# Which engine copies which accumulator at the end of a chunk, in an FFT and feed-forward kernel

## The chip, the cores and the metric

The kernel runs on one core of a Trainium2 chip. The metric is the device time of one execution in microseconds; a version is represented by the median of several runs. Lower is better. Five engines work side by side, each through its own queue in order: TensorE (PE in the profile; its weight loads are PEld), VectorE (DVE), ScalarE (ACT), GpSimd (POOL) and SyncE (SP), which issues most of the DMA transfers.

## The reference

The input `x` has shape 8 x 3008 x 256. The reference takes a two-dimensional Fourier transform over the last two axes, keeps the real part, and sends each of the 24064 rows through a feed-forward layer:

```python
X = np.fft.fft(np.fft.fft(x, axis=1), axis=2).real
h = X.reshape(-1, 256) @ w_in            # 256 -> 2048
g = where(h >= 1, h, where(h <= -1, 0, (h + 1)**2 / 4))
out = g @ w_out                          # 2048 -> 256
```

## The kernel before

The kernel splits the length 3008 into 64 x 47 and makes the transform of a batch by two stages of matmuls (`stage1`, `stage2`); the second transform is folded into `w_in`. Rows s and -s of the result are the sum and the difference of the same two products, so that only half of the rows is multiplied, and each product serves two signs (`sg` is 0 or 1). A batch has three chunks of columns, 482, 512 and 512 wide (`WIDTH`), and a chunk is worked through in 16 steps over the 2048 hidden features, 128 at a time. One such step is a unit `(b, k, f)`: batch, chunk, block of features. The first chunk of a batch is called narrow below, the other two wide.

For a unit, `gemm1` makes two products in PSUM (`uv`, three banks, six matmuls, L425). VectorE makes from them the two signs of h (`us` L428, `h` L430 and L431), ScalarE the square of the shifted half (`a`, L435 and L436), VectorE the activation (L447), ScalarE its high part (`gh`, L450) and POOL the low part (`gl`, L453). Four units later `gemm2` multiplies both parts with `w_out` (L485) and adds the products up in four PSUM accumulators of a bank each, `acc0` to `acc3`. Accumulator `dh * 2 + sg` holds half `dh` of the 256 output features for sign `sg`, and `gemm2` fills them in this order, three matmuls each. They are summed over the 16 units of a chunk. At the last unit the four sums are copied to SBUF (`o`), by VectorE (L496) or ScalarE (L494), and stored, one store for each `dh` (L503). The next chunk starts by overwriting the same four banks, so its first matmul into a bank waits until that bank's copy is over. Between the two stand the six `uv` matmuls of one unit and, in most batches, one piece of the next batch's FFT (`s`, L315 or L388).

The first batch differs. Its chunks are worked first over four units and later over the other twelve, while the weights are still being prepared. After the four units the sums are stored as parts (L501); after the twelve, VectorE adds the loaded parts to the accumulators (L492), all four of them.

What sets the order: for the first 24 units the order on each engine is pinned as written. After that the framework's scheduler orders each engine's queue when the program is built, by priority and by modelled times at which operands are ready. The copies are traced with a priority 150 steps ahead (`EVICT_AHEAD`), so that they may be queued ahead of work that is written earlier. FFT pieces of the next batch are spread over the units (`fft_pieces`), and the loads of x for it stand in SP's queue between the stores; POOL (and at times VectorE) adds them up (`fold_x`, L136 and L140).

Of the kernel before, what the change touches and what calls it, by code (L numbers as in the profile page):

```python
# [113 lines left out]
def fft_ffn_kernel(ctx: ExitStack, tc: tile.TileContext, x, cst, w_in, w_out, out):  # L114
# [296 lines left out]
    n_units = len(units)  # L411
# [50 lines left out]
    def gemm2(i):  # L462
        b, k, f = units[i]
        n = WIDTH[k]
        act = acts.pop(i)
        half_way = b == 0 and f == FIRST - 1
        begin, last = f == 0 or (b == 0 and f == FIRST), half_way or f == NFT - 1
        if begin:
            for j in range(4):
                accs[j] = ps.tile([P, CH], F32, tag=f"acc{j}", name=f"acc_{i}_{j}", bufs=1)  # L470
        for dh in range(2):
            wc = slice(dh * P, (dh + 1) * P)
            add = (k, dh) in outs if b == 0 else False
            if last:
                o = outs.pop((k, dh)) if add else sb.tile([P, 2, CH], F32, tag="o", name=f"o_{i}_{dh}", bufs=2)
            for sg in range(2):
                acc = accs[dh * 2 + sg]
                if i < NATIVE:
                    wo_at = (f % 2) * D + dh * P
                    terms = [(wo32[f // 2][:, wo_at : wo_at + P], act[0])]  # L480
                else:
                    gh, gl = act
                    terms = [(wo[t][:, f, wc], g) for t, g in (("woh", gh), ("wol", gh), ("woh", gl))]
                for j, (w, g) in enumerate(terms):
                    nc.tensor.matmul(  # L485
                        acc[:, :n], w, g[:, sg], start=(begin and j == 0), stop=(last and j == len(terms) - 1)
                    )
                if last:

                    with tc.high_priority(offset=EVICT_AHEAD):  # L490
                        if add:
                            nc.vector.tensor_tensor(o[:, sg, :n], acc[:, :n], o[:, sg, :n], op=ALU.add)  # L492
                        elif sg:
                            nc.scalar.activation(o[:, sg, :n], acc[:, :n], AF.Copy)  # L494
                        else:
                            nc.vector.tensor_copy(o[:, sg, :n], acc[:, :n])  # L496
                    if i == n_units - 1:
                        nc.sync.dma_start(out[b, k, dh, sg, :, :n], o[:, sg, :n])
            if half_way:
                parts[k, dh] = dr.tile([P, 2, CH], F32, tag="part", name=f"part_{k}_{dh}", bufs=6)  # L500
                nc.sync.dma_start(parts[k, dh][:, :, :n], o[:, :, :n])  # L501
            elif last and i < n_units - 1:
                nc.sync.dma_start(out[b, k, dh].rearrange("s p t -> p s t")[:, :, :n], o[:, :, :n])  # L503
# [75 lines left out]
    for i in range(n_units + LAG):  # L579
# [18 lines left out]
        if 2 <= i < PINNED and i not in SKIP:  # L598
            gemm2(second)
            second += 1  # L600
# [11 lines left out]
        if i >= PINNED:  # L612
            gemm2(second)
            second += 1
# [57 lines left out]
```

## Time and profile before

| | |
|---|---|
| median of 3 runs | 1746.41 us (1745.89 to 1746.51) |
| profiled execution | 1746.05 us |
| its span, first to last instruction | 1744.3 us |
| granted TensorE clock | 1.000 |
| copies on VectorE, L496 | 48, mean 672 ns, 32.0 us in all |
| copies on ScalarE, L494 | 48, mean 580 ns, 26.8 us in all |
| additions of the first batch on VectorE, L492 | 12, mean 676 ns, 7.5 us in all |
| L447 on VectorE | 360, mean 1518 ns |
| L450 on ScalarE | 360, mean 1045 ns |

A row of the waits names the waiting engine and line, what released it, the total in us, the number of times and the longest. A row in order of time gives the start in us, the duration in us, engine, line and operation, output and inputs, shape, and in brackets the idle time ahead of it and what ended that. A matmul is drawn longer than the distance to the next one, because matmuls overlap in the array and their ends are modelled; a merged row ends in the number of instructions that it holds. A wait for several things is put down to the one that came last.

### The profile page before, as it was taken

To read this page: it belongs to the slowest core of one execution; us is meant where nothing else is said; L and a number is where in the kernel's file an instruction comes from. 1 tells how busy PE (TensorE), PEld (TensorE's weight loads), DVE (VectorE), ACT (ScalarE), POOL (GpSimd) and SP (SyncE) were. 2 spreads that over 40 slices of the span, in tenths; PEclk is the share of its full clock that TensorE was granted. 3 is DMA by queue.
4 is the path that set the end of the run, shared out by engine and by line. 5 is a ranking of instruction groups with operands and counts; after the bars stand their busy time and mean duration, and the time that the engine had idled before them with its cause. 6 is when DMAs were issued, how large, how long until landed. Compare 5 with 4: busy or idle time off the path is not lost.

```text
span 1744.3 us, 21532 instructions
## 1 busy us (share of the span) xinstructions
PE 1729.2 (99%) x7818; PEld 1391.7 (80%) x7818; DVE 1419.8 (81%) x1752; ACT 1335.4 (77%) x1560; POOL 1156.8 (66%) x805
## 2 busy tenths in 40 slices
PE   9999999999999999999999999999999999999998
PEld 6556888888888888888888888887888878887876
DVE  7997788888887888777887888877888788788886
ACT  6877777877778777787777777778777787777775
POOL 1125867776678766777667766677666766667666
PEclk9999999999999999999999999999999999999999
DMA  8133112110011000110011100111001010000000
GB/s 316 47 108 130 57 48 73 48 37 31 13 61 59 31 25 23 50 59 31 25 46 39 59 19 25 49 37 59 31 13 37 1 36 31 0 25 24 1 25 25
DMA packets 33738, 80.89 MB, mean 46 GB/s; under 512 B 4704, under 2 KB 9952, under 8 KB 33632
## 3 DMA queue, kind: packets, MB, share of 16 engines
q1 hardware_dynamic: 33596, 79.52, 13.2%
q8 instruction: 61, 1.00, 0.2%
q14 instruction: 45, 0.37, 0.1%
q10 hardware_dynamic: 36, 0.01, 0.0%
HBM read 51.70 MB, written 27.81 MB: 46 GB/s over the span
## 4 chain that ended last, share of the span: by engine, by line
PE 65%; ACT 14%; DVE 8%; POOL 7%; issue 6%; DMA 0%; ACTq 0%; POOLq 0%; SPq 0%
PE acc L485 40%; PE uv L425 20%; POOL gl L453 7%; DVE h L447 6%; ACT a L436 5%; ACT gh L450 5%; ACT a L435 3%; PE s L315 2%; PE s L388 2%; PE wps L278 1%; DVE h L430 1%; ACT z L345 0%; DVE h L431 0%; DMA x<-in_x_dram 0%; POOL y L136 0%
## 5 line engine op out<-in xcount | busy, mean ns | idle before, releaser
L453 POOL TENSOR_TENSOR gl<-h,gh 128x512 fp32r<-128x512 f32 (+1 forms) x720 | 1034.0, 1458 | 441.9 <-ACT gh L450 413.0
L447 DVE SCALAR_TENSOR_TENSOR h<-a,h 128x1024 f32<-128x1024 f32 (+1 forms) x360 | 546.5, 1518 | 226.8 <-ACT a L436 225.5
L450 ACT ACTIVATE gh<-h 128x1024 fp32r<-128x1024 f32 (+1 forms) x360 | 376.1, 1045 | 345.9 <-DVE h L447 316.5
L485 PE MATMUL acc<-gh,woh 128*128 128x512 f32 (+1 forms) x1440 | 570.5, 396 | 4.5 <-DVE o L496 3.1
L485 PE MATMUL acc<-gl,woh 128*128 128x512 f32 (+1 forms) x1440 | 563.9, 392 | 0.9 <-POOL gl L453 0.9
L485 PE MATMUL acc<-gh,wol 128*128 128x512 f32 (+1 forms) x1440 | 560.8, 389 | 0.0
L435 ACT ACTIVATE a<-h,biases 128x1024 f32<-128x1024 f32 (+1 forms) x384 | 431.7, 1124 | 26.2 <-DVE h L431 24.1
L436 ACT ACTIVATE a<-a 128x1024 f32<-128x1024 f32 (+1 forms) x384 | 398.9, 1039 | 7.8
L485 PEld LDWEIGHTS acc<-gh,woh 128*128 128x128 f32 x1440 | 270.7, 188 | 63.9 <-DVE o L496 6.3
L485 PEld LDWEIGHTS acc<-gl,woh 128*128 128x128 f32 x1440 | 271.3, 188 | 58.6 <-POOL gl L453 2.2
L485 PEld LDWEIGHTS acc<-gh,wol 128*128 128x128 f32 x1440 | 270.7, 188 | 54.7
L425 PE MATMUL uv<-pqh,wh 128*128 128x512 f32 (+1 forms) x768 | 310.7, 405 | 1.6 <-DVE h L431 0.9
L430 DVE TENSOR_TENSOR h<-us,uv 128x512 f32<-128x512 f32 (+1 forms) x384 | 259.8, 677 | 62.5 <-POOL gl L453 20.6
L425 PE MATMUL uv<-pql,wh 128*128 128x512 f32 (+1 forms) x768 | 299.0, 389 | 0.0
L425 PE MATMUL uv<-pqh,wl 128*128 128x512 f32 (+1 forms) x768 | 298.9, 389 | 0.0
L428 DVE SCALAR_TENSOR_TENSOR us<-nyb,delta,uv 128x512 f32<-128x512 f32 (+1 forms) x384 | 279.2, 727 | 16.7 <-PE uv L425 16.6
L431 DVE TENSOR_TENSOR h<-us,uv 128x512 f32<-128x512 f32 (+1 forms) x384 | 256.4, 668 | 0.0
L425 PEld LDWEIGHTS uv<-pqh,wh 128*128 128x128 f32 x768 | 144.2, 188 | 45.8 <-DVE h L431 6.7
L425 PEld LDWEIGHTS uv<-pqh,wl 128*128 128x128 f32 x768 | 144.2, 188 | 33.6 <-issue 5.4
L425 PEld LDWEIGHTS uv<-pql,wh 128*128 128x128 f32 x768 | 144.1, 188 | 30.1 <-DVE pql L174 0.2
L136 POOL TENSOR_TENSOR y<-x 96x512 f32<-96x512 f32 x60 | 106.0, 1769 | 27.9 <-DMA x<-in_x_dram 15.9
L345 ACT ACTIVATE z<-s 64x192 f32<-64x192 f32 x242 | 82.2, 340 | 4.8 <-PE s L315 1.0
(65 smaller groups left out, 681.8 us busy)
## 6 DMA issues: line engine op xcount, KB each, us to landing
x<-in_x_dram SPq DMA_DIRECT2D x64, 512.0 KB, 3.5
out_dram<-o SPq DMA_DIRECT2D x26, 512.0 KB, 2.8
out_dram<-o SPq DMA_DIRECT2D x14, 482.0 KB, 2.9
nyb<-nyr SPq DMA_DIRECT2D x24, 256.0 KB, 3.2
raw<-in_moe_w_in_dram SPq DMA_DIRECT2D x4, 512.0 KB, 7.3
raw<-in_moe_w_out_dram SPq DMA_DIRECT2D x4, 512.0 KB
part<-o SPq DMA_DIRECT2D x4, 512.0 KB
os<-part SPq DMA_DIRECT2D x4, 512.0 KB, 5.8
```

Source lines behind the costliest of these rows:

```text
L136: first = engine.tensor_tensor(y, t[:96, 0], t[:96, 1], op=ALU.add)
L345: ins = nc.scalar.activation(dst, src, AF.Copy)
L425: nc.tensor.matmul(t[:, :n], w[m][:, cols], r[:, m, :n], start=(j == 0), stop=(j == 2))
L428: nc.vector.scalar_tensor_tensor(us, nyb[b, k][:, :n], delta[:, f : f + 1], uv[0], op0=ALU.mult, op1=ALU.add)
L430: nc.vector.tensor_tensor(h[:, 0], us, uv[1], op=ALU.subtract)
L431: nc.vector.tensor_tensor(h[:, 1], us, uv[1], op=ALU.add)
L435: nc.scalar.activation(a, h, AF.Relu, bias=half, scale=0.5)
L436: nc.scalar.activation(a, a, AF.Square)
L447: nc.vector.scalar_tensor_tensor(h, a, 1.0, h, op0=ALU.min, op1=ALU.max)
L450: nc.scalar.activation(gh, h, AF.Copy)
L453: nc.gpsimd.tensor_tensor(gl[:, sg], h[:, sg], gh[:, sg].bitcast(F32), op=ALU.subtract)
L485: nc.tensor.matmul(acc[:, :n], w, g[:, sg], start=(begin and j == 0), stop=(last and j == len(terms) - 1))
```

## The change

At the end of a chunk VectorE copied acc0 and acc2 (`sg` 0) and ScalarE acc1 and acc3 (`sg` 1). After the change VectorE copies acc0 and acc3, ScalarE acc1 and acc2. The very last unit of the kernel keeps the old division, and the additions of the first batch are untouched. This concerns 23 chunk ends: the three half-way ones of the first batch and 20 of the 21 chunks of the other seven.

```diff
                     with tc.high_priority(offset=EVICT_AHEAD):
                         if add:
                             nc.vector.tensor_tensor(o[:, sg, :n], acc[:, :n], o[:, sg, :n], op=ALU.add)
-                        elif sg:
+                        elif sg != (0 if i == n_units - 1 else dh):
                             nc.scalar.activation(o[:, sg, :n], acc[:, :n], AF.Copy)
                         else:
                             nc.vector.tensor_copy(o[:, sg, :n], acc[:, :n])
```

## The prediction

> **What bounds the kernel now.** I read the page first, then the list of waits, then the same list for the copies and their neighbours alone, then the instructions in order of time around single chunk changes. The page says that PE (TensorE) is busy all the time:
>
> ```profile
> span 1744.3 us, 21532 instructions
> ...
> PE 1729.2 (99%) x7818; PEld 1391.7 (80%) x7818; DVE 1419.8 (81%) x1752; ACT 1335.4 (77%) x1560; POOL 1156.8 (66%) x805
> ```
>
> A busy PE only shows that it has little room, not that it sets the pace. The list of waits (total us, times, longest) shows who waits for whom:
>
> ```profile
> ACT gh L450 <- DVE h L447: 316.5, 257, 2.7
> DVE h L447 <- ACT a L436: 225.5, 313, 2.7
> ...
> DVE us L428 <- PE uv L425: 16.6, 25, 2.4
> ...
> PE acc L485 <- DVE o L496: 3.1, 9, 0.7
> ```
>
> VectorE (DVE) and ScalarE (ACT) wait for each other hundreds of times; VectorE waits for a finished uv bank of TensorE 25 times in all. Asked of L428, the first VectorE step behind each pair of uv banks, for 500 to 1735 us alone, the view of one line gives:
>
> ```profile
> L428 DVE SCALAR_TENSOR_TENSOR us<-nyb,delta,uv x281: 702/734/745, 499.3 to 1725.3; 128x512 f32<-128x512 f32 x96, 128x482 f32<-128x482 f32 x45
> ...
> its engine sat idle before it (us, times) until:
> who waited for it (us, times):
>   PEld uv L425: 3.6, 11
> ```
>
> Nothing stands under "sat idle before it": in 281 units VectorE never once stood idle for TensorE here, while TensorE's weight loads waited 11 times for VectorE. The last L428 starts at 1725.3, so all 25 of those waits lie before 500 us. From 500 us on the pace is set by the loop L430, L431 (VectorE), L435, L436 (ScalarE), L447 (VectorE), L450 (ScalarE), L453 (POOL), and TensorE runs beside it with little to spare. A wait that TensorE loses is worth its time only where TensorE is about to fall behind that loop; a step that leaves the loop is worth its time wherever the loop has no other wait.
>
> **What is moved.** The copies that lie in 500 to 1735 us, by the view of their two lines:
>
> ```profile
> L496 DVE COPY o<-acc x34: 646/678/686, 552.7 to 1677.5; 128x512 f32<-128x512 f32 x22, 128x482 f32<-128x482 f32 x12
> ```
>
> ```profile
> L494 ACT ACTIVATE o<-acc x34: 557/579/601, 553.5 to 1678.7; 128x512 f32<-128x512 f32 x22, 128x482 f32<-128x482 f32 x12
> ```
>
> Two copies on each engine at each of 17 chunk changes, before and after: nothing is added or removed on either engine. The third accumulator (acc2) goes from VectorE to ScalarE, the fourth (acc3) the other way. Acc2 is complete three matmuls before acc3, and the next chunk wants it three matmuls earlier. What counts is where the second copy stands in each queue, and there are two pictures. The first is the change from the narrow chunk (482 columns) to the next one; ScalarE, VectorE, then TensorE:
>
> ```profile
> 552.42 1.04 ACT L436 ACTIVATE a<-a 128x1024 f32<-128x1024 f32 x1
> 553.49 1.04 ACT L494 ACTIVATE o<-acc 128x482 f32<-128x482 f32 x2
> 555.04 1.06 ACT L450 ACTIVATE gh<-h 128x1024 fp32r<-128x1024 f32 x1 [0.52 <-DVE h L447]
> ```
>
> ```profile
> 552.74 0.65 DVE L496 COPY o<-acc 128x482 f32<-128x482 f32 x1
> 553.50 1.45 DVE L447 SCALAR_TENSOR_TENSOR h<-a,h 128x1024 f32<-128x1024 f32 x1
> 554.88 0.65 DVE L496 COPY o<-acc 128x482 f32<-128x482 f32 x1
> ```
>
> ```profile
> 554.90 0.39 PE L485 MATMUL acc<-gl,woh 128*128 128x512 f32 x1
> 555.58 0.50 PE L485 MATMUL acc<-gh,woh 128*128 128x512 f32 x1 [0.28 <-DVE o L496]
> ```
>
> ScalarE makes its two copies back to back, 553.49 to 554.53. VectorE's second copy stands behind L447 and ends at 555.53; TensorE, which wants acc2, starts at 555.58. The second picture is a change between wide chunks, again ScalarE, VectorE, TensorE:
>
> ```profile
> 624.52 0.58 ACT L494 ACTIVATE o<-acc 128x512 f32<-128x512 f32 x1
> 626.30 1.06 ACT L450 ACTIVATE gh<-h 128x1024 fp32r<-128x1024 f32 x1 [1.20 <-DVE h L447]
> 627.26 0.58 ACT L494 ACTIVATE o<-acc 128x512 f32<-128x512 f32 x1
> 627.74 1.14 ACT L435 ACTIVATE a<-h,biases 128x1024 f32<-128x1024 f32 x1
> ```
>
> ```profile
> 624.65 1.56 DVE L447 SCALAR_TENSOR_TENSOR h<-a,h 128x1024 f32<-128x1024 f32 x1
> 626.13 0.68 DVE L496 COPY o<-acc 128x512 f32<-128x512 f32 x1
> 626.73 0.67 DVE L431 TENSOR_TENSOR h<-us,uv 128x512 f32<-128x512 f32 x1
> ```
>
> ```profile
> 627.19 0.40 PE L485 MATMUL acc<-gl,woh 128*128 128x512 f32 x1
> 627.42 0.40 PE L485 MATMUL acc<-gh,woh 128*128 128x512 f32 x1
> ```
>
> Here ScalarE's second copy stands behind L450 and pushes L435, the next step of the loop, to 627.74, although its input (L431) is there at 627.40. TensorE starts on acc2 at 627.42 without a wait: VectorE's copy is over at 626.81.
>
> **Each part, with its cost.** Narrow changes: TensorE's matmuls follow each other by 0.23 us (627.19 to 627.42), so 554.90 to 555.58 holds a loss of 0.68 - 0.23 = 0.45 us. If ScalarE copies acc2 in the second of its two places, acc2 is free at 554.53, and the loss goes. Next in line is acc3, wanted at 555.13 + 3 x 0.23 = 555.8 and free on VectorE at 555.53: no new wait. The loop gains nothing here, since ScalarE's pair stood ahead of L450 already and VectorE's place is the same.
>
> Wide changes: acc2 is ready three matmuls (0.7 us) before acc3 was. ScalarE stands idle for 1.20 us ahead of L450, so I expect the copy of acc2 in that gap, at about 625.0 to 625.6, with L450 still at 626.30, held by L447. Then L435 starts when L431 is done, at about 627.42 instead of 627.74: 0.32 us off the loop. It would be 0.47 if VectorE also put L431 ahead of its copy of acc3 (L435 then starts right behind L450, at 627.27), and nothing if the copy stayed behind L450. I take 0.32, the case that leaves VectorE's order as it is. It lies on the path because nothing else holds L435.
>
> The two changes of this kind in the last part, where there are no FFT pieces, are alike:
>
> ```profile
> 1544.74 0.58 ACT L494 ACTIVATE o<-acc 128x512 f32<-128x512 f32 x1
> 1545.22 1.09 ACT L435 ACTIVATE a<-h,biases 128x964 f32<-128x964 f32 x1
> ```
>
> ```profile
> 1544.26 0.64 DVE L431 TENSOR_TENSOR h<-us,uv 128x482 f32<-128x482 f32 x1
> ```
>
> L431 ends at 1544.90, so L435 gains 0.30 there. At the four changes that begin batches 3 to 6 (694, 906, 1118 and 1330 us) the gain is lost again: POOL stands for x from memory before it can feed the loop, and that fetch starts when POOL's own earlier step frees the buffer.
>
> ```profile
> 704.77 0.32 POOL L140 TENSOR_TENSOR yd<-x 96x64 f32<-96x64 f32 x1 [3.55 <-DMA x<-in_x_dram]
> ```
>
> The stores: the second one of a chunk waits for acc2 and acc3, and can leave up to 1.0 us earlier (626.81 instead of 627.84). Nobody gains: behind it in SP's queue stand loads that wait for POOL.
>
> ```profile
> SPq L128 <- POOL y L136: 750.0, 51, 56.4
> ```
>
> The changes before 500 us: three half-way ones in the first batch, where each engine makes both copies in a row and the order is fixed by hand, and three at 340, 412 and 482 us, where TensorE does not wait for a copy (the list for 500 to 1735 us alone has all nine waits for L496, 3.1 us). I cost them at nothing; what hides them is the FFT or weight matmuls that stand between two chunks there, and without that cover each would cost the 0.45 us above.
>
> The sum, for the loop: the wide changes inside batches at 624, 836, 1048, 1260 and 1471 us give 5 x 0.32 = 1.6 us, and those at 1541 and 1675 us 0.30 + 0.32 = 0.6; together 2.2 us. TensorE must follow. It loses 0.45 us at each narrow change now, and that goes, so it has 0.45 us more per batch while the loop asks for 0.32. The profiled execution took 1746.05 us, with 1.75 us around its span; 1746.05 - 2.2 = 1743.85. The median of the runs, 1746.41, is 0.36 above it, so the forecast for the median is 1744.2 us. With 0 and 0.47 in place of 0.32 the same sum gives 1746.4 and 1743.1.
>
> **Rival 1, TensorE is the bound after all.** Then every wait for acc2 counts. The nine waits for L496 sum to 3.1 us; each hides another 0.16 us (a matmul is drawn 0.39 long and followed after 0.23), which makes 4.5. One of the nine is for acc0, which stays on VectorE, 0.17 + 0.16 = 0.3:
>
> ```profile
> 1541.82 0.45 PE L485 MATMUL acc<-gh,woh 128*128 128x482 f32 x1 [0.17 <-DVE o L496]
> ```
>
> So 4.2 us go, and the time is 1742.2. For it speaks 99% busy; against it the empty list before L428. The Trainium skill (Trainium Kernel Development and Optimization, Performance Expectations) calls matmul busy time a bad metric for the distance to the limit, since matmuls are pipelined; the drawn 0.39 against a spacing of 0.23 agrees, and by it the 99% is no evidence for this rival.
>
> **Rival 2, nothing moves.** The copy of acc2 stays behind L450 at wide changes, or another wait of the loop takes up the 0.3 us: the loop's own waits above are 225.5 / 313 = 0.7 and 316.5 / 257 = 1.2 us each, and one of them need only grow. TensorE's gain at narrow changes and its loss at wide ones (acc2 free at 627.84, wanted at 627.42) cancel. The time is 1746.4, give or take 1.
>
> **Rival 3, slower.** The copy of acc2 is queued behind L450 at every change, narrow ones too. ScalarE keeps its order: ahead of 626.30 it stood idle for 1.20 us with a copy queued behind L450. Behind L450 a copy starts 0.1 us before L450's end (627.26), so acc2 is free at 556.0 + 0.58 = 556.6 at a narrow change instead of 555.53, 1.06 us more; at a wide change 627.84, 0.5 us late. With TensorE falling behind the loop, five of each make 5 x 1.06 + 5 x 0.5 = 7.8 us: 1754.2. It decides as soon as L450 stands ahead at the narrow changes; at wide ones alone it is rival 2. For it: L450 is ahead of ScalarE's second copy at wide changes now. Against it: acc2 is ready earlier than acc3, and the copies carry a raised priority. The Trainium skill (PSUM — Partial Sum Buffer, Engine vs sequencer instructions) says that the queues of these engines are strict FIFO; the 1.20 us ahead of L450 agrees. By that rule the copy pays for whatever stands ahead of it, and the change would be the 7.8 us slower if the order came out so.
>
> **How the numbers follow.** A measurement of this kernel can tell about 0.2% (3.5 us) from no change. Forecast: 0.48, of which a quarter goes to times under 1742.9, because L431 may also move and TensorE's own gain may add to it. Rival 1: 0.20, faster. Rival 2: 0.14, the same. Rival 3, with any other reordering of the loop that costs it one more wait per change: 0.18, slower. So faster is 0.20 + 0.12 = 0.32, the same 0.36 + 0.14 = 0.50, slower 0.18. The range leaves out rival 3 and reaches from a little below rival 1, 1741.8, to rival 2 with its 1 us and some, 1748.0.
>
> **What would show it.** Right: at 624 us and its four repeats ScalarE has its two copies together ahead of L450, and L435 starts 0.3 us after L450 ends or sooner; TensorE's waits for L496 fall from nine to four or fewer; the list before L428 gets a few waits for TensorE of 0.1 to 0.3 us. Wrong: L450 between ScalarE's two copies; waits of TensorE for L494 of about 1 us; L435 as late as now; or an order of the loop between two chunk changes that isn't the one of now, which no step above prices.

## The result and the profile after

The kernel after takes 1737.59 us (median of 5 runs, 1735.25 to 1739.35), the kernel before, run beside it, 1746.31 us (5 runs, 1744.97 to 1746.51): 8.7 us less, ratio 0.995, 95% interval 0.9939 to 0.996. The profiled execution took 1735.65 us, at a granted clock of 1.000. The forecast had 1744.2 us with a range of 1741.8 to 1748.0: the sign was right, the size was not, and the result lies below the range.

The page of the kernel after, its first lines:

```profile
span 1733.9 us, 21505 instructions
...
PE 1723.4 (99%) x7818; PEld 1394.8 (80%) x7818; DVE 1414.6 (82%) x1752; ACT 1332.6 (77%) x1560; POOL 1174.8 (68%) x805
```

The busy times hardly moved (VectorE 5 us less, ScalarE 3, POOL 18 more): no work left the kernel, so what changed is the waiting. The list of waits of the kernel after:

```profile
ACT gh L450 <- DVE h L447: 311.5, 285, 2.8
DVE h L447 <- ACT a L436: 234.4, 309, 2.2
...
DVE us L428 <- PE uv L425: 11.6, 13, 2.4
...
DVE h L430 <- POOL gl L453: 5.3, 8, 1.1
...
PE acc L485 <- DVE o L496: 1.8, 5, 0.6
```

TensorE's waits for a copy went from nine to five, against four or fewer in the forecast. Of the waits "POOL yd L140 <- DMA x", 15.7 us in five before, the four at the batch starts (14.6 us) are gone; one of 1.2 us before 300 us is left. The view of L428 for 500 to 1735 us in the kernel after has nothing under "sat idle before it" again, so TensorE still doesn't hold up VectorE:

```profile
L428 DVE SCALAR_TENSOR_TENSOR us<-nyb,delta,uv x280: 700/734/740, 502.4 to 1715.3; 128x512 f32<-128x512 f32 x96, 128x482 f32<-128x482 f32 x44
...
its engine sat idle before it (us, times) until:
who waited for it (us, times):
  DVE h L430: 1.0, 2
  PEld uv L425: 0.7, 3
```

The narrow change of the kernel after, TensorE in order of time; the first row overwrites acc1, the third acc2:

```profile
553.91 0.39 PE L485 MATMUL acc<-gh,woh 128*128 128x512 f32 x1
...
554.37 0.40 PE L485 MATMUL acc<-gl,woh 128*128 128x512 f32 x1
554.61 0.39 PE L485 MATMUL acc<-gh,woh 128*128 128x512 f32 x1
```

554.61 - 554.37 = 0.24: the 0.45 us that TensorE lost there before acc2 is gone, as forecast. The wide change of the kernel after, ScalarE and then VectorE:

```profile
623.23 1.07 ACT L494 ACTIVATE o<-acc 128x512 f32<-128x512 f32 x2
625.01 1.06 ACT L450 ACTIVATE gh<-h 128x1024 fp32r<-128x1024 f32 x1 [0.71 <-DVE h L447]
625.97 1.13 ACT L435 ACTIVATE a<-h,biases 128x1024 f32<-128x1024 f32 x1
```

```profile
623.36 1.55 DVE L447 SCALAR_TENSOR_TENSOR h<-a,h 128x1024 f32<-128x1024 f32 x1
624.83 0.67 DVE L431 TENSOR_TENSOR h<-us,uv 128x512 f32<-128x512 f32 x1
625.43 0.68 DVE L496 COPY o<-acc 128x512 f32<-128x512 f32 x1
```

ScalarE makes both copies ahead of L450 (before: one ahead, one behind), VectorE has L431 ahead of its second copy (before: behind), and L435 follows L450 at once, 2.74 us after the first copy's start; before that was 627.74 - 624.52 = 3.22. The last part looks the same (ScalarE in the kernel after):

```profile
1533.50 1.07 ACT L494 ACTIVATE o<-acc 128x512 f32<-128x512 f32 x2
1535.18 1.01 ACT L450 ACTIVATE gh<-h 128x964 fp32r<-128x964 f32 x1 [0.62 <-DVE h L447]
1536.10 1.09 ACT L435 ACTIVATE a<-h,biases 128x964 f32<-128x964 f32 x1
```

And POOL at the start of a batch, where it stood 3.55 us for x before:

```profile
698.92 2.23 POOL L136 TENSOR_TENSOR y<-x 96x512 f32<-96x512 f32 x1
701.40 3.33 POOL L453 TENSOR_TENSOR gl<-h,gh 128x482 fp32r<-128x482 f32 x2 [0.24 <-ACT gh L450]
704.81 0.32 POOL L140 TENSOR_TENSOR yd<-x 96x64 f32<-96x64 f32 x1
```

A pair of L453 now stands between L136, whose end releases the fetch of x, and yd (L140), which needs that x. The wait is covered.

The loads of x wait for POOL as before (SyncE's own queue in the kernel after):

```profile
SPq L128 <- POOL y L136: 745.2, 51, 56.7
```

POOL's move is not in the diff. When the two copies changed engines, the framework's scheduler put the queues of VectorE and ScalarE in another order at about 420 places, 33 of them with a copy in them and the others between the changes, mostly exchanges of neighbours (L431 with L447, L435 with L450), and moved yd on POOL at four batch starts. TensorE's and SyncE's queues stayed the same. Between the first copy (52.2 and 52.1 us) and the end of the span the kernel after is 10.3 us shorter. To see where they lie, take the start of VectorE's first copy at each chunk end, and the difference from one to the next. Stretch a lies between the ends of the narrow and the first wide chunk of a batch, b between those of the two wide chunks, c is the narrow chunk of the next batch, in which yd stands; each is the mean of three batches, 553 to 1189 us before. "Narrow, no yd" is the narrow chunk from 1331 to 1400 us before, which is like c but has no yd in it; "last" is what follows up to the end of the last narrow chunk, 1400 to 1607 us:

| kernel | a | b | c | narrow, no yd | last |
|---|---|---|---|---|---|
| before | 71.18 | 70.33 | 70.55 | 69.25 | 207.16 |
| after | 71.64 | 69.98 | 69.02 | 69.31 | 203.78 |
| copies ahead alone (below) | 71.14 | 70.02 | 71.60 | 68.73 | 206.63 |
| POOL's move alone | 71.17 | 70.34 | 69.55 | 69.24 | 207.12 |
| both | 71.21 | 70.01 | 69.65 | 68.76 | 206.64 |
| both, and L431 ahead | 71.04 | 69.81 | 69.30 | 68.60 | 206.47 |

The kernel after is 1.5 us faster in c, 0.35 in b, 3.4 in the last stretch, and 0.46 slower in a. The forecast had b, and 0.6 us of the last stretch (the changes at 1471 and 1541 us); it had nothing in a and c.

### The profile page after: what moved, and what is told of

Read it like the earlier page. It is cut to its first block, busy times and chain, and to the rows that moved or that the text cites. A ratio compares the mean times of both kernels' runs of the same rounds, so it can differ in the third digit from the quotient of the medians.

```text
span 1733.9 us, 21505 instructions
## 1 busy us (share of the span) xinstructions
PE 1723.4 (99%) x7818; PEld 1394.8 (80%) x7818; DVE 1414.6 (82%) x1752; ACT 1332.6 (77%) x1560; POOL 1174.8 (68%) x805
## 3 DMA queue, kind: packets, MB, share of 16 engines
q1 hardware_dynamic: 33596, 79.52, 13.3%
## 4 chain that ended last, share of the span: by engine, by line
PE 79%; ACT 11%; DVE 6%; issue 2%; POOL 1%; DMA 0%; ACTq 0%; SPq 0%; POOLq 0%
PE acc L485 49%; PE uv L425 24%; DVE h L447 5%; ACT a L436 4%; ACT gh L450 4%; ACT a L435 3%; PE s L315 3%; PE s L388 2%; PE wps L278 1%; POOL gl L453 1%; DVE h L431 0%; ACT z L345 0%; DMA raw<-in_moe_w_in_dram 0%; DVE h L430 0%; DVE o L496 0%
## 5 line engine op out<-in xcount | busy, mean ns | idle before, releaser
L453 POOL TENSOR_TENSOR gl<-h,gh 128x512 fp32r<-128x512 f32 (+1 forms) x720 | 1050.1, 1480 | 428.0 <-ACT gh L450 381.5
L447 DVE SCALAR_TENSOR_TENSOR h<-a,h 128x1024 f32<-128x1024 f32 (+1 forms) x360 | 539.9, 1500 | 237.0 <-ACT a L436 234.4
L450 ACT ACTIVATE gh<-h 128x1024 fp32r<-128x1024 f32 (+1 forms) x360 | 376.2, 1045 | 340.6 <-DVE h L447 311.5
L435 ACT ACTIVATE a<-h,biases 128x1024 f32<-128x1024 f32 (+1 forms) x384 | 431.1, 1123 | 24.2 <-DVE h L431 22.8
L436 ACT ACTIVATE a<-a 128x1024 f32<-128x1024 f32 (+1 forms) x384 | 398.7, 1038 | 7.6
L430 DVE TENSOR_TENSOR h<-us,uv 128x512 f32<-128x512 f32 (+1 forms) x384 | 260.0, 677 | 52.2 <-POOL gl L453 5.3
L428 DVE SCALAR_TENSOR_TENSOR us<-nyb,delta,uv 128x512 f32<-128x512 f32 (+1 forms) x384 | 278.6, 725 | 11.7 <-PE uv L425 11.6
L431 DVE TENSOR_TENSOR h<-us,uv 128x512 f32<-128x512 f32 (+1 forms) x384 | 256.2, 667 | 0.0
L136 POOL TENSOR_TENSOR y<-x 96x512 f32<-96x512 f32 x60 | 108.0, 1803 | 27.7 <-DMA x<-in_x_dram 11.8
```

What stands on the lines that cost most here:

```text
L136: first = engine.tensor_tensor(y, t[:96, 0], t[:96, 1], op=ALU.add)
L428: nc.vector.scalar_tensor_tensor(us, nyb[b, k][:, :n], delta[:, f : f + 1], uv[0], op0=ALU.mult, op1=ALU.add)
L430: nc.vector.tensor_tensor(h[:, 0], us, uv[1], op=ALU.subtract)
L431: nc.vector.tensor_tensor(h[:, 1], us, uv[1], op=ALU.add)
L435: nc.scalar.activation(a, h, AF.Relu, bias=half, scale=0.5)
L436: nc.scalar.activation(a, a, AF.Square)
```

## The experiments

Every kernel below has the order of all five queues written out: each instruction of a queue is tied to the one ahead of it, by a dependency without a semaphore, so that the scheduler has no choice left. The edit is the same each time, and only the lists and the line that divides the copies differ:

```diff
+    known = {ins.name: ins for ins in traced}
+    for text in _ORDER.values():
+        row = [known[f"I-{n}"] for n in _order_of(text) if f"I-{n}" in known]
+        for first, after in zip(row, row[1:]):
+            dep = mybir.DependencyInfo(mybir.DependencyClass.NoSync, mybir.DependencyReason.DATA)
+            tc.add_manual_dep(after, first.name, dep, reason="given order")
```

The short diffs below show the queue at one of the places meant, as lines of the kernel in order. "Less before" is the median less that of the kernel before, run beside them (1746.17 us beside kernels 1 to 4, 1746.61 beside 5 to 8, 1745.65 beside 9 to 12).

| kernel | median us | less before | ratio, 95% interval |
|---|---|---|---|
| 1 new division, old order | 1746.94 | +0.8 | 1.0002, 0.9993 to 1.0011 |
| 2 old division, new order | 1736.73 | -9.4 | 0.9946, 0.9933 to 0.9958 |
| 3 before, yd moved | 1741.93 | -4.2 | 0.9976, 0.9967 to 0.9985 |
| 4 after, yd back | 1745.01 | -1.2 | 0.9991, 0.9982 to 1.0 |
| 5 copies ahead alone | 1746.59 | 0.0 | 1.0003, 0.9994 to 1.0012 |
| 6 as 5, yd moved | 1738.37 | -8.2 | 0.9954, 0.9941 to 0.9966 |
| 7 as 6, L431 ahead | 1736.66 | -10.0 | 0.9944, 0.9931 to 0.9956 |
| 8 after, changes as before | 1746.69 | +0.1 | 0.9999, 0.999 to 1.0007 |
| 9 as 5, L447 behind L136 | 1741.68 | -4.0 | 0.9974, 0.9963 to 0.9984 |
| 10 as 7, last batch of after | 1733.55 | -12.1 | 0.9927, 0.9914 to 0.9939 |
| 11 as 10, narrow stretches too | 1732.86 | -12.8 | 0.9922, 0.9908 to 0.9935 |
| 12 as 11, yd one pair further | 1732.36 | -13.3 | 0.992, 0.9906 to 0.9933 |

**1. The new division in the old order.** The copies of acc2 and acc3 take each other's places, and nothing else moves. ScalarE at a wide change:

```diff
-L494(acc1) L450 L494(acc3) L435
+L494(acc1) L450 L494(acc2) L435
```

> The new division of the copies in the queue orders of the kernel before: every engine's order is fixed as it was, the copy of acc2 takes the place that the copy of acc3 had on ScalarE, and the other way round on VectorE. Theory O (the time came from the queues that the scheduler ordered anew): no gain, 1746 us give or take 2. Theory C (it came from who copies what): about 1738 us. The forecast's rival 2 says 1746.

No gain. This is the first form of the forecast's second rival (the copy stays behind L450), as a kernel. ScalarE in it, and TensorE's row for acc2:

```profile
627.41 1.06 ACT L450 ACTIVATE gh<-h 128x1024 fp32r<-128x1024 f32 x1 [1.20 <-DVE h L447]
628.38 0.58 ACT L494 ACTIVATE o<-acc 128x512 f32<-128x512 f32 x1
```

```profile
629.01 0.50 PE L485 MATMUL acc<-gh,woh 128*128 128x512 f32 x1 [0.79 <-ACT o L494]
```

TensorE waits 0.79 us for acc2 behind L450, and it costs nothing; TensorE isn't what sets the pace.

**2. The old division in the new order.** The opposite: the line of the diff is undone, and the queues are those of after, with acc2 and acc3 exchanged.

```diff
-                        elif sg != (0 if i == n_units - 1 else dh):
+                        elif sg:
```

> The old division of the copies in the queue orders of the kernel after: the copy of acc3 takes the place of acc2's on ScalarE (ahead of L450), and acc2's the place behind L431 on VectorE. Theory O: most of the gain is there, 1738 to 1741 us; up to 3 us more than the kernel after, because TensorE wants acc2 0.7 us earlier than acc3 and VectorE's second place is the later one. Theory C: 1746 us.

All of the gain. So it isn't who copies what that counts, but where the second copy, of whichever accumulator, stands in ScalarE's queue, and what else the scheduler moved.

**3 and 4. POOL's move alone, and all but POOL's move.** POOL at the start of a batch, in the third kernel; the fourth has the opposite edit on the kernel after.

```diff
-L136 L140(yd) L453 L453
+L136 L453 L453 L140(yd)
```

> The kernel before with one thing of the kernel after: on POOL, at the start of four batches, the small subtraction for the FFT (L140), which waits 3.5 us for x from memory, stands behind one more pair of L453. All else in the order of before. Theory P (POOL's wait for x was what each batch lost): TensorE's waits for uv behind it go, 0.95 us in each of three or four batches, and the time is 1742 to 1743.5 us. Theory V (it is the order on VectorE and ScalarE): 1746 us.

> The kernel after with the small subtraction (L140) back at its old place on POOL, ahead of the pair. All else as after. Theory P: the wait of 3.5 us for x is back and about half of the gain is gone, 1741 to 1743 us. Theory V: 1738 us, no change from the kernel after.

Moving yd alone is worth 4.2 us, in c only (70.55 to 69.55 in the table, and 70.79 to 69.60 in the first such stretch: 4.2 in all). Within the new order it is worth more, 8.7 - 1.2 = 7.5 us: the effects don't add up, and something that the copies gain is lost where yd waits.

**5. The forecast's picture alone.** ScalarE's copy of acc2 goes ahead of L450; POOL and everything else stay.

```diff
-L494(acc1) L450 L494(acc2) L435
+L494(acc1) L494(acc2) L450 L435
```

> New division; every queue in the order of before, with one thing moved: at 20 chunk changes ScalarE's copy of acc2 stands directly behind its copy of acc1, ahead of L450 (VectorE's copy of acc3 stands where that of acc2 stood, POOL is as before). This is the picture that the forecast priced, by itself. By the forecast's sum: 2.2 us under the kernel before, 1744.0 us (median of the kernel before in its call less 2.2), batch periods shorter by 0.3 us each. By the theory that the gain lies in other places of the order than the copies: the same as the kernel with the old order and the new division, 1746 to 1747 us, since the 0.3 us at a change is met again by the loop's next wait; TensorE's waits for L494 of 0.7 to 1.8 us that were seen there must go in both cases.

No gain in all, though locally the forecast's 0.32 us is there, and c takes it back. ScalarE in this kernel:

```profile
624.39 1.06 ACT L494 ACTIVATE o<-acc 128x512 f32<-128x512 f32 x2
626.15 1.06 ACT L450 ACTIVATE gh<-h 128x1024 fp32r<-128x1024 f32 x1 [0.70 <-DVE h L447]
627.29 1.15 ACT L435 ACTIVATE a<-h,biases 128x1024 f32<-128x1024 f32 x1
```

L435 starts 627.29 - 624.39 = 2.90 us after the first copy, 0.32 sooner than before (3.22), and stretch b is 70.33 - 70.02 = 0.31 shorter. But c is 1.05 us longer, so that the batches with a yd lose 0.7 us each, and those without gain. The rows of POOL and of VectorE at the batch start, in the kernel before:

```profile
699.93 1.29 POOL L136 TENSOR_TENSOR y<-x 96x512 f32<-96x512 f32 x1
```

```profile
700.08 2.16 DVE L447 SCALAR_TENSOR_TENSOR h<-a,h 128x964 f32<-128x964 f32 x1 [0.57 <-ACT a L436]
```

and in this kernel:

```profile
699.52 2.21 POOL L136 TENSOR_TENSOR y<-x 96x512 f32<-96x512 f32 x1
705.57 0.33 POOL L140 TENSOR_TENSOR yd<-x 96x64 f32<-96x64 f32 x1 [3.83 <-DMA x<-in_x_dram]
```

```profile
699.39 1.18 DVE L447 SCALAR_TENSOR_TENSOR h<-a,h 128x964 f32<-128x964 f32 x1 [0.30 <-ACT a L436]
```

The two instructions don't run side by side: the one that starts second takes about 1 us more. Before, L136 started 0.15 us ahead of L447. The 0.3 us gained on the loop brings L447 0.13 us ahead of L136, L136 takes 2.21 us in place of 1.29, and the fetch of x that its end releases leaves 0.9 us later, counted from L136's start. So yd starts at 705.57 us in place of 704.77, although the loop came earlier, and the next L453 stands behind it. The same happens at 912 and 1125 us (L136 2.22 us each).

**6. Both moves.**

```diff
-L136 L140(yd) L453 L453
+L136 L453 L453 L140(yd)
```

> The kernel with the copies ahead of L450, and with POOL's small subtraction (L140) behind one more pair of L453 at four batch starts, as in the kernel after. That move alone gave 4.2 us. If the places at the changes and the wait for x add up as the forecast has them (0.32 us at each wide change, and at the four batch starts too, where the forecast took the gain as lost): 4.2 + 2.2 + 4 x 0.32 = 7.7 us under before, 1738.5 us. If the copies' place is worth nothing: 1742 us, as with POOL's move alone.

8.2 us less, where 7.7 was worked out from the forecast's 0.32 us at eleven wide changes and POOL's 4.2. Once nothing stands behind the fetch, the copies' place is worth 8.2 - 4.2 = 4.0 us; L136 still takes 2.2 us here, and it no longer matters.

**7 and 8. The places at the changes, and the places between them.** The seventh kernel has the order of after in the 33 places in which a copy takes part, the eighth in the 388 others; both have POOL's order of after. What the seventh adds to the sixth is on VectorE:

```diff
-L447 L496(acc3) L431
+L447 L431 L496(acc3)
```

> New division; VectorE's and ScalarE's order of after where a copy takes part in the difference (33 places: ScalarE's two copies ahead of L450, VectorE's L431 ahead of its second copy), the order of before everywhere between; POOL's order of after. If what is left of the gain (about 4.5 us beside POOL's move) comes from the places at the changes: 1737.5 us, as after. If it comes from the order between the changes: 1742 us, as with POOL's move alone. A share of each gives a time between.

> The complement: new division, the order of before where a copy takes part (ScalarE's copy of acc2 behind L450 at wide changes, VectorE's copy of acc3 ahead of L431), the order of after at the 388 other places of VectorE's and ScalarE's queues and on POOL. If the order between the changes carries what is left: 1737.5 us, or up to 0.8 us per wide change more where TensorE waits for acc2 (at most 1743). If the places at the changes carry it: 1742 us or more.

The seventh gains 10.0 us, as much as the kernel after or more; L431 ahead gives 10.0 - 8.2 = 1.7 us, and 0.47 - 0.32 = 0.15 at eleven wide changes makes 1.65. The sums agree by luck in part: stretch a gains 0.17 too, and at 424 us, where one L447 takes 2.36 us for 1.24, about 1.1 us is lost again (the last section has the cause). The eighth gains nothing, not even POOL's 4.2 us: the new order between the changes goes badly with the copies behind L450. Its c is 70.44 and its narrow stretch without yd 71.43, 1.4 and 2.1 us longer than in the kernel after, with TensorE waiting 0.4 to 1.9 us for L494 at seven wide changes. About 1.1 us in the narrow stretch without yd, and in one of the three c (71.18 us; the other two take 70.06 and 70.08), is a single L447 of 2.6 us for 1.46 (at 1381 and 956 us; the last section has the cause). What loses the other 1.0 us in each isn't known.

**9. The collision taken out.** The fifth kernel, where L447 waits for L136 at the three batch starts:

```diff
+    for vector, pool in [(5900, 6149), (7738, 7987), (9576, 9825)]:
+        dep = mybir.DependencyInfo(mybir.DependencyClass.Sync, mybir.DependencyReason.DATA)
+        tc.add_manual_dep(known[f"I-{vector}"], f"I-{pool}", dep, reason="behind POOL's addition")
```

> The kernel with the copies ahead of L450 and POOL's order of before (it took as long as before), with one thing more: at the three batch starts (about 700, 912 and 1125 us) VectorE's L447 that met POOL's L136 there now waits for it. There L447 had begun 0.13 us ahead of L136, L136 took 2.21 us in place of 1.29, and so the fetch of x that follows L136, and yd (L140) behind it, came 0.9 us later than in the kernel before. If that is where the gain of the copies' place went: L136 takes 1.29 us again, yd starts 0.9 us earlier after the batch's start, and the time falls by 3 x 0.9 = 2.7 us, to about 1743.9 us, near the forecast. If the copies' place has no worth while POOL waits for x: the same 1746.6 us, or more by the added wait of VectorE, up to 1 us at each of three places.

POOL and then VectorE in this kernel:

```profile
699.64 1.31 POOL L136 TENSOR_TENSOR y<-x 96x512 f32<-96x512 f32 x1
704.43 0.32 POOL L140 TENSOR_TENSOR yd<-x 96x64 f32<-96x64 f32 x1 [3.48 <-DMA x<-in_x_dram]
```

```profile
700.99 1.16 DVE L447 SCALAR_TENSOR_TENSOR h<-a,h 128x964 f32<-128x964 f32 x1 [1.76 <-POOL y L136]
```

VectorE stands idle for 1.76 us, and yet the kernel is 4.0 us faster than before: L136 takes 1.31 us, yd starts 1.1 us sooner. That is more than the 2.7 us expected. Of the difference to the fifth kernel the profiles show 1.8 us in two of the three narrow stretches (71.63 to 70.77 and 71.45 to 70.49; at the first, 71.73 to 71.60, a stall of TensorE of 1.07 us at 729.7 takes it back) and 1.2 us at 1470 to 1539 us, which the edit doesn't touch. Both of these odd pieces are one L447 that runs 1.1 us longer in one of the two kernels (last section). Without the stall the three narrow stretches would have gained about 3.1 us, an estimate from these figures, near the 2.7 expected; the rest is chance that the edit doesn't control.

**10 to 12. Where the order between the changes helps.** The seventh kernel with the order of after also between the changes from 1323 us on (the expectation names 1391; the narrow stretch between takes 68.69 us for 68.60, so nothing hangs on it); then also in the narrow stretches behind 480 us; then with yd behind a second pair of L453. ScalarE in the last batch, where the queue differs first behind the wide change:

```diff
-L435 L436 L435 L436 L450
+L435 L436 L435 L450 L436
```

> The kernel with the order of after at the changes and on POOL and the order of before between the changes, with the order of after also between the changes behind 1391 us (168 places in all). Its last batch took 206.5 us by the order of before between the changes, that of after 203.8. If that is the order between the changes of the last batch alone: 2.7 us less, about 1734.0 us. If the last batch gains from what the earlier batches leave behind: as that kernel, 1736.7 us.

> As the kernel with the last batch's order of after, and the order of after between the changes also in the four stretches of narrow chunks behind 480 us (256 places in all). In after these stretches are 0.1 to 0.5 us shorter, and the first wide stretch of each batch, which keeps the order of before here, is 0.5 us longer than with that. If the stretches are independent: 0.3 us for each of four, about 1732.8 us. If the shorter narrow stretch is paid by what follows: 1734 us or more.

> As the kernel before it in this call, with POOL's yd (L140) behind one more pair of L453 at the four batch starts. With the order of after yd still waited 0.1 to 0.6 us for x. If that wait is on the path: up to 1.1 us less, about 1731.7 us. If not, or if yd behind the second pair delays L136 behind it as much: no difference to the other kernel.

The tenth gains 12.1 us, 2.1 more than the seventh; its last stretch is 203.84 us, that of after 203.78. ScalarE in the seventh and in the tenth kernel:

```profile
1537.90 1.10 ACT L435 ACTIVATE a<-h,biases 128x964 f32<-128x964 f32 x1
1539.03 1.01 ACT L436 ACTIVATE a<-a 128x964 f32<-128x964 f32 x1
1539.95 0.99 ACT L450 ACTIVATE gh<-h 128x964 fp32r<-128x964 f32 x1
```

```profile
1535.86 1.10 ACT L435 ACTIVATE a<-h,biases 128x964 f32<-128x964 f32 x1
1537.43 1.01 ACT L450 ACTIVATE gh<-h 128x964 fp32r<-128x964 f32 x1 [0.46 <-DVE h L447]
1538.34 0.99 ACT L436 ACTIVATE a<-a 128x964 f32<-128x964 f32 x1
```

L450, for which POOL waits, starts 2.05 us behind L435 with L436 ahead of it and 1.57 without: POOL's next L453 gets its input 0.5 us sooner, though ScalarE now stands idle for 0.46 us. There is a second difference: behind 1400 us the seventh kernel has four L447 of more than 2.3 us, the tenth none. That the order shortens the last stretch is shown there (206.47 to 203.84 us, while the intervals of the two kernels as a whole just overlap); how much of it each of the two differences carries isn't. The eleventh kernel (1732.86 us) and the twelfth (1732.36) cannot be told apart; both beat the kernel after, whose interval (0.9939 to 0.996) lies above theirs. The eleventh takes 68.55 us for c. Of the 0.1 to 0.6 us that yd waited in the seventh, 0.14 us at 494 us and 0.06 at 703 are left in the eleventh and nothing at the other two batch starts, so the twelfth had next to nothing to take away: it doesn't show whether such a wait costs time.

## Why the prediction was wrong

**What bounds the kernel: right.** The loop sets the pace from 500 us on. Kernels 1 and 2 have the waits of TensorE that the first rival counts, at wide changes in the one and at narrow ones in the other (matmuls up to 1.8 and 1.2 us late); the one takes as long as before, the other has all of the gain. So rival 1 falls, and the nothing that was put down for the narrow changes stands.

**The wide changes inside the batches: right, to the hundredth.** 0.32 us at a change (kernel 5: 0.32 by the rows, 0.31 by stretch b); the forecast's other case, 0.47 with L431 ahead, is what the kernel after has (0.48 by the rows). Rival 3 falls with it, and rival 2 as a time: ScalarE has both copies ahead of L450 at all twenty changes from 340 to 1667 us. But the second form of rival 2, "another wait of the loop takes up the 0.3 us", is what kernel 5 shows where the copies alone move: the wait is POOL's for x. The change at 412 us was put at nothing, hidden by other matmuls; the stretch behind it gains 0.28 us (70.27 in kernel 3, 69.99 in kernel 6).

**The batch starts: the step that failed.** "At the four changes that begin batches 3 to 6 (694, 906, 1118 and 1330 us) the gain is lost again: POOL stands for x from memory before it can feed the loop, and that fetch starts when POOL's own earlier step frees the buffer." The mechanism is there, but it was used for the wrong term, in three ways. It took yd's place on POOL as given, and the kernel after has it one pair later, which alone is worth 4.2 us (kernel 3) and stands nowhere in the sum. It took the loss as the 0.32 us of that one change; with yd at its old place such a stretch is 1.05 us longer, against 0.35 us that a and b gain (kernel 5), because the gain itself makes L447 meet L136 the other way round (kernel 9). And at 1330 us there is no such wait: the four are at 493, 700, 912 and 1125 us, and the narrow stretch from 1331 us gained 0.52 us in kernel 5.

**The sum.** Had the queues stayed as they were but for the copies, the time would have been 1746.6 us (kernel 5), not 1744.2. The 8.7 us come out of the kernels as follows: POOL's move 4.2, ScalarE's copy ahead of L450 4.0 more (the forecast's 0.32 us at eleven wide changes makes 3.5, and 412 us adds 0.28), L431 ahead 1.7, together 10.0 by the medians; by the profiled executions, from the first copy on, 4.2, 2.9 and 1.5, together 8.7. The 2.9 holds one L447 of 2.58 us (at 933 us, in the c of 70.36 us that raises kernel 6's mean); without its 1.1 us it is 4.0 too. What the order between the changes adds to that isn't settled in sum: by the medians the kernel after is 1.2 us slower than kernel 7, by the profiles 1.6 us faster, and the intervals overlap. In parts it gains 2.7 us in the last stretch and, each time, 0.3 in c, and loses 0.6 in a, 0.2 in b and 0.7 in the narrow stretch without yd. The forecast's last paragraph names "an order of the loop between two chunk changes that isn't the one of now, which no step above prices". That is what happened, on POOL above all. It had a chance only as a loss, within rival 3's 0.18; as a gain it had neither chance nor price.

**The last part.** The change at 1471 us gives 0.32 us in kernel 5, as priced (69.81 to 69.49); those at 1541 and 1675 us, priced at 0.30 and 0.32, give 0.17 and 0.19 (66.15 to 65.98 and 61.61 to 61.42). Of the 3.4 us that the kernel after gains in its last stretch, 2.7 come with the order between the changes (kernel 10).

What stays open is about 1.0 us of the eighth kernel's loss in each narrow stretch, and what decides at each place which of L447 and L453 goes first (last section). A fifth buffer for x, which might take away yd's wait whatever the order, wasn't tried.

## What to carry to other kernels

Where a scheduler orders the queues, moving an instruction to another engine is a change to the order of everything near it in modelled time: compare the queues engine by engine, before believing that an effect belongs to the line that was edited, and pin the old order to measure the line alone. A gain on the loop reaches the end only if nothing between follows another clock: look for the waits on memory along the way (the 3.55 us of POOL for x was one row of the list) and first ask what may be put under them. And a fetch that starts when a buffer comes free starts when the instruction that frees it ends, so that instruction's duration is on the path even where its engine isn't busy.

## What the runs showed of the hardware

VectorE's L447 and POOL's L136 exclude each other. With L136 ahead by 0.15 us it takes 1.29 us and L447 2.16; with L447 ahead by 0.13 us it takes 1.18 us and L136 2.21; apart, in kernel 9, they take 1.16 and 1.31. So whichever starts second pays about 0.9 to 1 us, and a shift of 0.3 us decided who. The Trainium skill (SBUF — State Buffer, Who interferes with whom) says that a VectorE instruction with two inputs in SBUF and a GpSimd instruction that reads SBUF share one port as an exclusive lock, and that the order of issue decides which of the two is blocked until the other has finished. Both instructions are of that kind (L447 reads a and h, L136 two halves of x). The numbers agree to 0.15 us: one strictly after the other, L447 would have ended at 699.93 + 1.29 + 1.16 = 702.38 in the kernel before, and it ended at 702.24. What the forecast could have taken from the row of before is that L447 with 2.16 us, beside 1.15 for the next one of the same shape, was already paying for the lock.

The same goes for L447 and L453, which reads h and gh. L453 comes in pairs, and L447 often starts while the first of a pair runs. Kernel 5 and then kernel 9, at the same place:

```profile
726.72 3.41 POOL L453 TENSOR_TENSOR gl<-h,gh 128x482 fp32r<-128x482 f32 x2
727.58 1.45 DVE L447 SCALAR_TENSOR_TENSOR h<-a,h 128x964 f32<-128x964 f32 x1 [1.20 <-ACT a L436]
```

```profile
725.58 2.43 POOL L453 TENSOR_TENSOR gl<-h,gh 128x482 fp32r<-128x482 f32 x2
726.44 2.59 DVE L447 SCALAR_TENSOR_TENSOR h<-a,h 128x964 f32<-128x964 f32 x1 [1.19 <-ACT a L436]
```

L447 starts 0.86 us behind the pair in both. In kernel 5 it gets in between the two L453, and the second one pays; in kernel 9 both L453 go first, L447 ends 1.1 us later, and TensorE's stall at 729.7 us follows. The 1.2 us at 1470 to 1539 us are the same: in kernel 9 L447 starts 0.14 us ahead of an L453 and takes 1.25 us, in kernel 5 the two start within 0.01 us and it takes 2.38. Nothing in the edit reaches these places, so steps of about 1.1 us in one profile can be chance. Their number follows the order too: L447 takes more than 2.3 us 21 times in the kernel before and in kernel 7, 7 times in the kernel after and 9 in kernel 8. And a busy time holds such waiting: all L447 together take 546.5 us before and 539.9 after, more than the 5 us by which VectorE's busy time fell.
